# Zero products in TensorE's gaps, one engine for the later preparation, and earlier weight loads in a fused linear-attention and MLP kernel

## The chip, the cores and the metric

The kernel runs on one core of one Trainium2 chip. The metric is device time in microseconds, the median of several runs. A profile of one execution is shown beside it; its span is the time between the first and the last recorded instruction. Engines: TensorE (PE; PEld is its weight load), VectorE (DVE), ScalarE (ACT), GpSimd (POOL), SyncE (SP, which here only issues DMAs).

## The reference

Two parts follow one another: a recurrent linear attention with a per-channel decay, and an MLP with a squared ReLU.

```python
# attention: batch 4, heads 8, sequence 768, head_dim 48
for t in range(S):
    cur = einsum('bhd,bhe->bhde', u * kt, vt)
    y[:, :, t] = einsum('bhd,bhde->bhe', rt, state + cur)
    state = w[None, :, :, None] * state + einsum('bhd,bhe->bhde', kt, vt)
# x: 3072 tokens x 384 (heads side by side)
h = x @ w_in                 # 384 -> 2048
g = maximum(h, 0) ** 2
out = g @ w_out              # 2048 -> 384
```

## The kernel before

The sequence is cut into 6 chunks of 128 steps; with 4 batches this makes 24 **units**, numbered n = 4 x chunk + batch. A unit takes its steps in this order:

- SyncE loads `kt`, `rt`, `vt` of [128, 8, 48] F32 (L209), five buffers each. One queue carries these loads and the stores of the output (L408), in order.
- Preparation: `rk` = r*k (L214, GpSimd only); `rku` = rk*u (L217); `kw` = k times a decay factor, into the padded bf16 tile `kp` (L220); `rw` = r times a decay factor, into `rp` (L223); `vb` = v in bf16 (ScalarE, L226); `du` = sum of rku (VectorE, L228); `dv` = v*du (L231). `rku`, `kw`, `rw` and `dv` may go to GpSimd or VectorE. There are three padded tiles each, so the names kp_77, kp_78, kp_79 are units 0, 1, 2 modulo 3, and likewise rp_74, rp_75, rp_76.
- TensorE transposes kp and rp into a bf16 PSUM tile (L241), ScalarE copies it out as `rkT` (L247), TensorE forms k v (L258) for the state; VectorE adds it to the old state (L268, L270), VectorE or GpSimd multiplies with the decay (L277), ScalarE casts it to bf16 (L279).
- TensorE forms the scores (L288) into two PSUM tiles `at0`, `at1`, VectorE masks them (L298, `AT`), TensorE forms y from the state and the scores (L308, L313), VectorE adds dv (L321, `yb`), TensorE transposes y (L331), ScalarE copies it to `xt` (L352).

The MLP runs over **groups** of units: units 0 and 1, units 2 and 3, then four units at a time. For each group 16 hidden chunks are formed: three products of 128 x 256 or 128 x 512 columns (L363), ReLU on VectorE (L374) or ScalarE (L376), square on ScalarE (L381) or GpSimd (L383). Then for each unit the output is summed over the 16 chunks in four parts of four products (L396), copied by ScalarE (L404) and stored.

The weights are cast to bf16 by DMAs that GpSimd issues, four parts of `w_in` (L187) and four of `w_out` (L191). Part i is ordered behind `rk` of unit `W_IN_AT[i]` or `W_OUT_AT[i]`.

The order on every engine is written by a **planner**, a list scheduler that runs when the program is built. Every step is an `Op` with a duration for each engine that may do it ("T" TensorE, "V" VectorE, "A" ScalarE, "P" GpSimd, "D" the DMA engines, "S" the stores), a due time (6.6 us per unit, `PACE`), its dependences and the buffers that it takes. The planner repeatedly places the step that can start first (ties by due time; an engine that is not a step's first one is charged 8 us). The instructions are then emitted in that order. Each engine runs its queue in order, so a step that waits holds everything behind it. PSUM has three rings: `a` (3 tiles, attention), `h` (3, hidden chunks), `o` (2, output); `ps_tile` opens a tile of a ring when the first product of a step is emitted.

Before all units, a short prologue builds the decay factors. `emit_wc` transposes the decay row `wrow` on TensorE (L166) and squares it seven times on VectorE (L171).

Of the kernel before, what the change touches and what calls it, by code (L numbers as in the profile page):

```python
# [8 lines left out]
F32 = mybir.dt.float32  # L9
BF16 = mybir.dt.bfloat16  # L10
# [5 lines left out]
def kernel(  # L16
# [11 lines left out]
    nc = tc.nc  # L28
# [15 lines left out]
    const = ctx.enter_context(tc.tile_pool(name="const", bufs=1))  # L44
    work = ctx.enter_context(tc.tile_pool(name="work", bufs=1))
    psum = ctx.enter_context(tc.tile_pool(name="psum", bufs=1, space=bass.MemoryType.PSUM))
# [5 lines left out]
        out=wb, in_=bass.AP(tensor=w.tensor, offset=w.offset, ap=[[0, 128], [1, HD]])  # L52
# [10 lines left out]


    class Op:
        __slots__ = ("eng", "key", "deps", "takes", "emit", "start", "end", "lat", "by", "home")

        def __init__(self, eng, key, deps, takes, emit, lat=0.15):
            self.eng, self.key, self.deps, self.takes, self.emit = eng, key, deps, takes, emit
# [8 lines left out]
    rings = {}  # L78
# [4 lines left out]
    def sb_ring(name, bufs, shape, dt):  # L83
        ring(name, bufs, lambda i: work.tile(shape, dt, name=name, tag=name, bufs=bufs))
# [4 lines left out]
    def op(eng, key, deps, emit, takes=(), uses=(), lat=0.15):  # L89
        o = Op(eng, key, [d for d in deps if d is not None], list(takes), emit, lat)  # L90
        for b in list(takes) + list(uses):
            b.users.append(o)
        ops.append(o)
        return o
# [2 lines left out]
        return Buf(ringname)  # L97

    NLOAD, NPADS = 5, 3
    sb_ring("kt", NLOAD, [C, H, D], F32)  # L100
    sb_ring("rt", NLOAD, [C, H, D], F32)
    sb_ring("vt", NLOAD, [C, H, D], F32)
# [17 lines left out]
    for nm in ("rp", "kp"):  # L120
        pads[nm] = []
        for i in range(NPADS):
            t = const.tile([C, H, PAD], BF16, name=f"{nm}{i}")
# [5 lines left out]

    def ps_tile(buf, shape, dt):  # L130
        buf.tile = psum.tile(shape, dt, name=f"ps_{buf.ring}", tag=f"ps_{buf.ring}", bufs=rings[buf.ring]["bufs"])
        return buf.tile


    iota_i = const.tile([128, 1], mybir.dt.int32)
# [26 lines left out]
        nc.scalar.activation(wr.rearrange("p h d -> p (h d)"), lnw, AF.Exp, scale=er)  # L162

    def emit_wc():
        wcol_p = psum.tile([128, NP], F32, name="ps_a", tag="ps_a", bufs=rings["a"]["bufs"])
        nc.tensor.transpose(wcol_p, wrow.rearrange("p i d -> p (i d)"), ident4)  # L166
        wcs = const.tile([128, NP], F32, name="wsq", bufs=2)
        nc.vector.tensor_copy(wcs, wcol_p)
        for _ in range(C.bit_length() - 1):
            sq = const.tile([128, NP], F32, name="wsq", bufs=2)  # L170
            nc.vector.tensor_tensor(sq, wcs, wcs, ALU.mult)  # L171
            wcs = sq
        for i in range(2):
            rows = slice(i * PAD, i * PAD + D)
            nc.vector.tensor_copy(wc[rows, :, i, :], wcs[rows, :, None].to_broadcast([D, NP, D]))

    nc.scalar.dma_start(
        out=ub, in_=bass.AP(tensor=u.tensor, offset=u.offset, ap=[[0, 128], [1, HD]])
    )
    o_wk = op({"A": 1.95}, -50, [], emit_wk, lat=0.0)  # L180
    o_wr = op({"A": 0.6}, -49, [o_wk], emit_wr)
# [15 lines left out]
    for n in range(NU):  # L197
        c, b = divmod(n, B)
        t0 = c * C
        q = dict(n=n)  # L200
        units.append(q)
        K = PACE * n
        bufs = {nm: take(nm) for nm in ("kt", "rt", "vt", "vb", "rk", "rku", "du", "dv", "kp", "rp", "rkT", "AT", "yb")}
        q["b"] = bufs
        T = lambda nm, bufs=bufs: bufs[nm].tile

        def load(e, q=q, b=b, t0=t0, T=T):
            for nm, src in (("kt", k), ("rt", r), ("vt", v)):
                nc.sync.dma_start(out=T(nm), in_=src[b, :, t0 : t0 + C, :].rearrange("h t d -> t h d"))  # L209

        q["load"] = op({"D": 3.4}, K, [], load, takes=[bufs["kt"], bufs["rt"], bufs["vt"]], lat=1.4)
        two = lambda f: (lambda e: f({"P": nc.gpsimd, "V": nc.vector}[e]))
        q["rk"] = op({"P": 1.0}, K + 1, [q["load"]],
                     two(lambda e, T=T: e.tensor_tensor(T("rk"), T("rt"), T("kt"), ALU.mult)),  # L214
                     takes=[bufs["rk"]], uses=[bufs["rt"], bufs["kt"]])
        q["rku"] = op({"P": 1.0, "V": 0.47}, K + 2, [q["rk"]],
                      two(lambda e, T=T: e.tensor_tensor(T("rku"), T("rk"), ub, ALU.mult)),  # L217
                      takes=[bufs["rku"]], uses=[bufs["rk"]])
        q["kw"] = op({"P": 1.0, "V": 0.47}, K + 0.1, [q["load"], o_wk],
                     two(lambda e, T=T: e.tensor_tensor(T("kp")[:, :, :D], T("kt"), wk, ALU.mult)),  # L220
                     takes=[bufs["kp"]], uses=[bufs["kt"]])
        q["rw"] = op({"P": 1.0, "V": 0.47}, K + 0.2, [q["load"], o_wr],
                     two(lambda e, T=T: e.tensor_tensor(T("rp")[:, :, :D], T("rt"), wr, ALU.mult)),  # L223
                     takes=[bufs["rp"]], uses=[bufs["rt"]])
        q["vb"] = op({"A": 0.51}, K + 0.3, [q["load"]],
                     lambda e, T=T: nc.scalar.copy(T("vb"), T("vt")), takes=[bufs["vb"]], uses=[bufs["vt"]])  # L226
        q["du"] = op({"V": 0.55}, K + 3, [q["rku"]],
                     lambda e, T=T: nc.vector.tensor_reduce(T("du"), T("rku"), axis=mybir.AxisListType.X, op=ALU.add),  # L228
                     takes=[bufs["du"]], uses=[bufs["rku"]])
        q["dv"] = op({"P": 0.83, "V": 0.47}, K + 4, [q["du"], q["vb"]],  # L230
                     two(lambda e, T=T: e.tensor_tensor(T("dv"), T("vb"), T("du")[:, :, None].to_broadcast([C, H, D]), ALU.mult)),  # L231
                     takes=[bufs["dv"]], uses=[bufs["du"], bufs["vb"]])

# [16 lines left out]
        if not last:  # L250
            kv_p = take("a")
            sm = take(f"sm{b}")
            sb = take(f"sb{b}")

            def kvm(e, T=T, kv_p=kv_p):
                t = ps_tile(kv_p, [128, NP, 2, D], F32)
                for p in range(NP):
                    nc.tensor.matmul(  # L258
                        out=t[:, p], lhsT=T("kp")[:, 2 * p : 2 * p + 2, :],
                        rhs=T("vb")[:, 2 * p : 2 * p + 2, :], start=True, stop=True,  # L260
                    )

            q["kvm"] = op({"T": 0.2}, K + 1.2, [q["kw"], q["vb"], q["trr"]], kvm, takes=[kv_p, sm], uses=[bufs["kp"], bufs["vb"]], lat=0.3)
            old = units[n - B]["sm"] if c else None

            def sadd(e, kv_p=kv_p, sm=sm, old=old):
                if old is None:
                    nc.vector.tensor_tensor(sm.tile, kv_p.tile, wc, ALU.mult)  # L268
                else:
                    nc.vector.tensor_tensor(sm.tile, kv_p.tile, old.tile, ALU.add)  # L270

            q["sm"] = sm
            q["smo"] = op({"V": 0.55}, K + 3, [q["kvm"], units[n - B]["smo"] if c else None], sadd,
                          uses=[sm, kv_p] + ([old] if old else []))
            if c:
                q["smo"] = op({"P": 1.0, "V": 0.47}, K + 5, [q["smo"]],
                              two(lambda e, sm=sm: e.tensor_tensor(sm.tile, sm.tile, wc, ALU.mult)), uses=[sm])  # L277
            q["sbo"] = op({"A": 0.51}, K + 6, [q["smo"]],
                          lambda e, sm=sm, sb=sb: nc.scalar.copy(sb.tile, sm.tile), takes=[sb], uses=[sm])  # L279
            q["sb"] = sb  # L280
# [54 lines left out]

    groups = [[0, 1], [2, 3]] + [list(range(i, i + B)) for i in range(B, NU, B)]
    o_win, o_wout = [], []
    W_IN_AT, W_OUT_AT = (0, 1, 1, 2), (3, 4, 5, 6)
    for dst, when, part in ((o_win, W_IN_AT, w_in_part), (o_wout, W_OUT_AT, w_out_part)):
        for i in range(PARTS):  # L340
            key = PACE * when[i] + 1.1 + 0.01 * i
# [74 lines left out]
    while left:  # L416
        best = None
        for o in left:
            t = 0.0
            okay = True  # L420
            for d in o.deps:
                if d.end is None:
                    okay = False
                    break
                t = max(t, d.end + d.lat)
            if not okay:
                continue
            for bf in o.takes:
                rg = rings[bf.ring]
                same = [x for x in o.takes if x.ring == bf.ring]  # L430
                i = len(rg["order"]) + same.index(bf) - rg["bufs"]
                if i >= 0:
                    if i >= len(rg["order"]):
                        okay = False
                        break
                    for x in rg["order"][i].users:
                        if x.end is None:
                            okay = False
                            break
                        t = max(t, x.end + 0.1)  # L440
            if not okay:
                continue
            for e in o.eng:
                s = max(t, free[e])
                away = AWAY.get(e, 0.0) if len(o.eng) > 1 and e != o.home else 0.0
                rank = (s, o.key + away)
                if best is None or rank < best[0]:
                    best = (rank, o, e)
        (s, _), o, e = best
        o.start, o.end, o.by = s, s + o.eng[e], e  # L450
        free[e] = o.end
        for bf in o.takes:
            rings[bf.ring]["order"].append(bf)
        left.remove(o)
        placed.append(o)

    for o in placed:
        for bf in o.takes:
            rg = rings[bf.ring]
            if rg["make"] is not None:  # L460
                bf.tile = rg["make"](rg["order"].index(bf))
        o.emit(o.by)


# [28 lines left out]
```

## Time and profile before

| | us |
|---|---|
| median of 3 runs (lowest to highest) | 207.88 (207.57 to 207.95) |
| the profiled execution, whole | 206.22 |
| its span | 204.0 |
| TensorE busy (1529 products) | 175.2 |
| VectorE busy (260 instructions) | 153.5 |
| ScalarE busy (240) | 127.6 |
| GpSimd busy (136) | 126.3 |
| mean granted TensorE clock | 0.971 |

Busy times are of one execution, and a TensorE that is busy is not at its peak: products are pipelined and their recorded ends are modelled. Durations below come from this execution. Its whole time is 2.2 us longer than its span and 1.66 us shorter than the median.

The larger groups of the page (line, engine, operation, result and inputs, count, busy us, mean ns, idle before and what ended it):

```profile
L374 DVE TENSOR_SCALAR gr<-ps_h 128x512 f32<-128x512 f32 (+1 forms) x78 | 46.7, 609 | 26.4 <-PE ps_h L363 21.9
L298 DVE TENSOR_TENSOR AT<-ps_a,smask 128x512 bf16<-128x512 f32 x48 | 30.9, 679 | 2.7 <-PE ps_a L288 2.4
L214 POOL TENSOR_TENSOR rk<-rt,kt 128x384 f32<-128x384 f32 x24 | 27.3, 1144 | 4.5 <-DVE wsq L171 4.0
```

Other groups mix several buffers of one kind. The prediction takes the preparation steps from the windows instead.

### The profile page before, as it was taken

The page shows a single profiled execution, that of the slowest core. Times are in us where ns is not written, and L with a number is a line of the kernel's source. Part 1 is how long each engine was busy: PE and PEld are TensorE (multiplying, and loading weights), DVE is VectorE, ACT ScalarE, POOL GpSimd, SP SyncE. Part 2 cuts the span into 40 slices and gives each one's busy share as a digit, 9 for nine tenths or more (in the row PEclk, how much of TensorE's full clock was granted, in tenths as well). Part 3 has the DMA queues.
Part 4 walks back from the last instruction along what each step waited for, and adds up shares of the span by engine and source line. Part 5 has one row for each costly group of instructions (what it writes and reads, how often), then busy time and mean ns, then how long its engine had stood idle before and what let it go on. Part 6 is the DMA issues. An engine that isn't in the chain of part 4 may idle for free.

```text
span 204.0 us, 4084 instructions
## 1 busy us (share of the span) xinstructions
PE 175.2 (86%) x1529; PEld 106.4 (52%) x1529; DVE 153.5 (75%) x260; ACT 127.6 (63%) x240; POOL 126.3 (62%) x136
## 2 busy tenths in 40 slices
PE   0147893999599999977999999799999999999992
PEld 0135561576356656553565655465556655555551
DVE  4899689478859999899989999999764564455200
ACT  3536475569553997965988777687566755544211
POOL 2767489548899698999998899995322020422200
PEclk9999999589969999999999999999999999999998
DMA  5999999981519989989815661110111011111122
GB/s 113 205 198 195 194 201 174 219 146 26 70 45 233 244 163 216 194 203 183 160 41 117 150 121 42 39 39 3 39 39 42 0 39 43 39 39 39 42 77 77
DMA packets 82367, 22.68 MB, mean 111 GB/s; under 512 B 75436, under 2 KB 82348, under 8 KB 82348
## 3 DMA queue, kind: packets, MB, share of 16 engines
q1 hardware_dynamic: 78480, 19.08, 42.6%
q0 software_dynamic: 3712, 3.15, 10.4%
q8 instruction: 12, 0.20, 0.4%
q10 hardware_dynamic: 156, 0.20, 0.4%
q14 instruction: 7, 0.06, 0.1%
HBM read 20.84 MB, written 4.72 MB: 125 GB/s over the span
## 4 chain that ended last, share of the span: by engine, by line
PE 66%; DVE 20%; DMA 6%; issue 3%; POOL 3%; ACT 1%; POOLq 0%; DVEq 0%; ACTq 0%
PE ps_o L396 27%; PE ps_h L363 26%; DMA w_out_sb<-in_moe_w_out_dram 4%; PE ps_a L241 4%; DVE AT L298 3%; PE ps_a L288 3%; PE ps_a L313 2%; DMA wrow<-in_w_dram 2%; DVE rku L217 2%; DVE gr L374 2%; PE ps_a L331 2%; PE ps_a L308 2%; DVE dv L231 2%; DVE rp_75 L223 1%; DVE yb L321 1%
## 5 line engine op out<-in xcount | busy, mean ns | idle before, releaser
L374 DVE TENSOR_SCALAR gr<-ps_h 128x512 f32<-128x512 f32 (+1 forms) x78 | 46.7, 609 | 26.4 <-PE ps_h L363 21.9
L363 PEld LDWEIGHTS <-w_in_sb 128*128 128x128 bf16 x336 | 31.2, 101 | 22.7 <-issue 3.0
L298 DVE TENSOR_TENSOR AT<-ps_a,smask 128x512 bf16<-128x512 f32 x48 | 30.9, 679 | 2.7 <-PE ps_a L288 2.4
L214 POOL TENSOR_TENSOR rk<-rt,kt 128x384 f32<-128x384 f32 x24 | 27.3, 1144 | 4.5 <-DVE wsq L171 4.0
L247 ACT COPY rkT<-ps_a 128x1024 bf16<-128x1024 bf16 x24 | 24.2, 1010 | 6.1 <-PE ps_a L241 6.1
L376 ACT ACTIVATE gr<-ps_h 128x512 f32<-128x512 f32 (+1 forms) x34 | 17.8, 532 | 8.0 <-PE ps_h L363 7.6
L404 ACT COPY osb<-ps_o 128x384 f32<-128x384 f32 x24 | 11.4, 475 | 15.2 <-PE ps_o L396 15.0
L383 POOL TENSOR_TENSOR g_2830<-gr 128x512 bf16<-128x512 f32 x5 | 5.2, 1039 | 20.6 <-DVE gr L374 20.6
L231 POOL TENSOR_TENSOR dv<-vb,du 128x384 f32<-128x384 bf16 x16 | 13.7, 857 | 5.4 <-DVE yb L321 2.4
L321 DVE TENSOR_TENSOR yb<-ps_a,dv 128x384 bf16<-128x384 f32 x24 | 13.1, 548 | 2.0 <-PE ps_a L313 2.0
L313 PE MATMUL ps_a<-vb,AT 128*128 128x48 bf16 x192 | 12.6, 190 | 1.5 <-DVE AT L298 1.5
L363 PE MATMUL ps_h<-xt_1214,w_in_sb 128*128 128x512 bf16 x48 | 12.5, 379 | 1.2 <-DVE gr L374 1.2
L288 PE MATMUL ps_a<-rkT 48*128 48x128 bf16 x192 | 10.7, 233 | 3.1 <-ACT rkT L247 3.1
L396 PE MATMUL ps_o<-w_out_sb,g_2035 128*128 128x384 bf16 x64 | 13.0, 326 | 0.0
L228 DVE TENSOR_REDUCE du<-rku 128x8 f32<-128x384 f32 x24 | 12.9, 539 | 0.1
L396 PE MATMUL ps_o<-w_out_sb,g_1046 128*128 128x384 bf16 x64 | 12.9, 326 | 0.0
L313 PEld LDWEIGHTS <-AT 128*128 128x128 bf16 x192 | 10.6, 101 | 4.3 <-DVE AT L298 2.3
L396 PE MATMUL ps_o<-w_out_sb,g_2479 128*128 128x384 bf16 x64 | 12.9, 326 | 0.0
L363 PE MATMUL ps_h<-xt_2112,w_in_sb 128*128 128x512 bf16 x48 | 12.8, 379 | 0.0
L363 PE MATMUL ps_h<-xt_2535,w_in_sb 128*128 128x512 bf16 x48 | 12.8, 379 | 0.0
L363 PE MATMUL ps_h<-xt_1707,w_in_sb 128*128 128x512 bf16 x48 | 12.7, 380 | 0.0
L396 PE MATMUL ps_o<-w_out_sb,g_1578 128*128 128x384 bf16 x64 | 12.5, 326 | 0.0
(180 smaller groups left out, 404.7 us busy)
## 6 DMA issues: line engine op xcount, KB each, us to landing
kt<-in_k_dram SPq DMA_DIRECT2D x24, 192.0 KB, 3.7
rt<-in_r_dram SPq DMA_DIRECT2D x24, 192.0 KB, 3.7
vt<-in_v_dram SPq DMA_DIRECT2D x24, 192.0 KB, 4.2
out_dram<-osb SPq DMA_DIRECT2D x24, 192.0 KB, 1.9
w_in_sb<-in_moe_w_in_dram POOLq DMA_DIRECT2D x4, 384.0 KB, 6.3
w_out_sb<-in_moe_w_out_dram POOLq DMA_DIRECT2D x4, 384.0 KB, 6.9
wb<-in_w_dram SPq DMA_DIRECT2D x1, 192.0 KB, 3.6
ub<-in_u_dram ACTq DMA_DIRECT2D x1, 192.0 KB, 3.9
```

What stands on the lines that cost most here:

```text
L214: two(lambda e, T=T: e.tensor_tensor(T("rk"), T("rt"), T("kt"), ALU.mult)),
L228: lambda e, T=T: nc.vector.tensor_reduce(T("du"), T("rku"), axis=mybir.AxisListType.X, op=ALU.add),
L231: two(lambda e, T=T: e.tensor_tensor(T("dv"), T("vb"), T("du")[:, :, None].to_broadcast([C, H, D]), ALU.mult)),
L247: lambda e, T=T, rk_p=rk_p: nc.scalar.copy(T("rkT"), rk_p.tile),
L288: nc.tensor.matmul(out=ts[i][:, p, :], lhsT=T("rkT")[rows, p, 1, :], rhs=T("rkT")[rows, p, 0, :], start=True, stop=True,)
L298: lambda e, T=T, i=i, x=x: nc.vector.tensor_tensor(T("AT")[:, i], x.tile, smask[:, None, :].to_broadcast([128, NP, C]), ALU.mult),
L313: nc.tensor.matmul(out=t[:, p, i, :], lhsT=T("AT")[:, i, p, :], rhs=T("vb")[:, 2 * p + i, :], start=st is None, stop=True, skip_group_chec ...
L321: lambda e, T=T, y_p=y_p: nc.vector.tensor_tensor(T("yb"), y_p.tile.rearrange("t p i d -> t (p i d)"), T("dv").rearrange("t h d -> t (h d) ...
L363: nc.tensor.matmul(out=t, lhsT=w_in_sb[:, kk, f * 128 : (f + 1) * 128], rhs=xt.tile[:, kk].rearrange("p b t -> p (b t)"), start=(kk == 0), ...
L374: nc.vector.tensor_scalar(gr.tile[:, : L * C], h.tile, 0.0, None, ALU.max)
L376: nc.scalar.activation(gr.tile[:, : L * C], h.tile, AF.Relu)
L396: nc.tensor.matmul(out=o_p.tile, lhsT=g.tile[:, f, j, :], rhs=w_out_sb[:, f, :], start=(f == 0), stop=(f == NF - 1),)
```

## The change

There are four edits.

1. A tile `zb` of zeros is set once. `warm` emits products of zeros into a given PSUM tile. In the prologue nine of them (`WARM0`) go ahead of the transpose of `wrow` and six (`WARM1`) behind it, into a tile of ring `a` of their own.
2. The planner notes for each TensorE step, if it is placed before 70 us of its own time, the gap that TensorE has in front of it. When such a step opens an F32 PSUM tile, `int(gap * 0.6 / 0.2133)` zero products are emitted into that tile first. The step's own first product starts the sum afresh. A step that opens two tiles (the scores) emits them for each. Steps that open a bf16 tile or none get no zeros.
3. For units from 8 on, `rku`, `kw`, `rw`, `dv` and the decay of the state are offered to GpSimd only. For units 0 to 7 VectorE's duration in the planner goes from 0.47 to 0.6.
4. The parts of w_in are ordered behind units 0, 0, 1, 1 instead of 0, 1, 1, 2, those of w_out behind 3, 3, 4, 4 instead of 3, 4, 5, 6.

```diff
+    WARM0, WARM1 = 9, 6
+    WARM_END = 70.0
+    NDVE = 8
...
     def ps_tile(buf, shape, dt):
         buf.tile = psum.tile(shape, dt, name=f"ps_{buf.ring}", tag=f"ps_{buf.ring}", bufs=rings[buf.ring]["bufs"])
+        if dt == F32 and now["gap"] > 0:
+            warm(buf.tile, shape, int(now["gap"] * FILL / 0.2133))
         return buf.tile
+    FILL = 0.6
+    now = dict(gap=0.0)
+    zb = const.tile([128, 512], BF16)
+    nc.vector.memset(zb, 0.0)
+
+    def warm(tile_, shape, count):
+        dims = list(shape[1:])
+        for _ in range(count):
+            nc.tensor.matmul(
+                out=tile_, lhsT=zb[:, :128], rhs=view(zb, dims), start=True, stop=True, skip_group_check=True
+            )
...
     def emit_wc():
+        first = psum.tile([128, 512], F32, name="ps_a", tag="ps_a", bufs=rings["a"]["bufs"])
+        warm(first, [128, 512], WARM0)
         wcol_p = psum.tile([128, NP], F32, name="ps_a", tag="ps_a", bufs=rings["a"]["bufs"])
         nc.tensor.transpose(wcol_p, wrow.rearrange("p i d -> p (i d)"), ident4)
+        warm(first, [128, 512], WARM1)
...
+        both = (lambda p_, v_, n=n: {"P": p_, "V": v_} if n < NDVE else {"P": p_})
...
-        q["rku"] = op({"P": 1.0, "V": 0.47}, K + 2, [q["rk"]],
+        q["rku"] = op(both(1.0, 0.6), K + 2, [q["rk"]],
...
-        q["dv"] = op({"P": 0.83, "V": 0.47}, K + 4, [q["du"], q["vb"]],
+        q["dv"] = op(both(0.83, 0.6), K + 4, [q["du"], q["vb"]],
...
-    W_IN_AT, W_OUT_AT = (0, 1, 1, 2), (3, 4, 5, 6)
+    W_IN_AT, W_OUT_AT = (0, 0, 1, 1), (3, 3, 4, 4)
...
         o.start, o.end, o.by = s, s + o.eng[e], e
+        o.gap = s - free[e] if e == "T" and s < WARM_END else 0.0
...
+        now["gap"] = o.gap
         o.emit(o.by)
```

`kw`, `rw` and the decay of the state (L277) are changed like `rku`. `view` gives the zeros the shape of the tile.

More of the change, by code (lines that the diff above doesn't have):

```diff
@@ L65 @@
     class Op:
-        __slots__ = ("eng", "key", "deps", "takes", "emit", "start", "end", "lat", "by", "home")
+        __slots__ = ("eng", "key", "deps", "takes", "emit", "start", "end", "lat", "by", "home", "gap")
         def __init__(self, eng, key, deps, takes, emit, lat=0.15):
@@ L131, in ps_tile, with view @@
         buf.tile = psum.tile(shape, dt, name=f"ps_{buf.ring}", tag=f"ps_{buf.ring}", bufs=rings[buf.ring]["bufs"])
+        if dt == F32 and now["gap"] > 0:
+            warm(buf.tile, shape, int(now["gap"] * FILL / 0.2133))
         return buf.tile
+    FILL = 0.6
[8 more added lines that the diff above has]
+            )
+    def view(t, dims):
+        cols = 1
+        for d in dims:
+            cols *= d
+        if len(dims) == 1:
+            return t[:, :cols]
+        if len(dims) == 2:
+            return t[:, :cols].rearrange("p (a b) -> p a b", a=dims[0])
+        return t[:, :cols].rearrange("p (a b c) -> p a b c", a=dims[0], b=dims[1])
     iota_i = const.tile([128, 1], mybir.dt.int32)
@@ L215 @@
                      takes=[bufs["rk"]], uses=[bufs["rt"], bufs["kt"]])
-        q["rku"] = op({"P": 1.0, "V": 0.47}, K + 2, [q["rk"]],
+        q["rku"] = op(both(1.0, 0.6), K + 2, [q["rk"]],
                       two(lambda e, T=T: e.tensor_tensor(T("rku"), T("rk"), ub, ALU.mult)),
                       takes=[bufs["rku"]], uses=[bufs["rk"]])
-        q["kw"] = op({"P": 1.0, "V": 0.47}, K + 0.1, [q["load"], o_wk],
+        q["kw"] = op(both(1.0, 0.6), K + 0.1, [q["load"], o_wk],
                      two(lambda e, T=T: e.tensor_tensor(T("kp")[:, :, :D], T("kt"), wk, ALU.mult)),
                      takes=[bufs["kp"]], uses=[bufs["kt"]])
-        q["rw"] = op({"P": 1.0, "V": 0.47}, K + 0.2, [q["load"], o_wr],
+        q["rw"] = op(both(1.0, 0.6), K + 0.2, [q["load"], o_wr],
                      two(lambda e, T=T: e.tensor_tensor(T("rp")[:, :, :D], T("rt"), wr, ALU.mult)),
@@ L275 @@
             if c:
-                q["smo"] = op({"P": 1.0, "V": 0.47}, K + 5, [q["smo"]],
+                q["smo"] = op(both(1.0, 0.6), K + 5, [q["smo"]],
                               two(lambda e, sm=sm: e.tensor_tensor(sm.tile, sm.tile, wc, ALU.mult)), uses=[sm])
```

## The prediction

> **What bounds the kernel now.** I read the page's 40 slices first, then the chain that ended last, then windows, waits and single instructions. Columns of a slice row: one digit per 5.1 us.
>
> ```profile
> PE   0147893999599999977999999799999999999992
> DVE  4899689478859999899989999999764564455200
> POOL 2767489548899698999998899995322020422200
> PEclk9999999589969999999999999999999999999998
> ...
> PE 66%; DVE 20%; DMA 6%; issue 3%; POOL 3%; ACT 1%; POOLq 0%; DVEq 0%; ACTq 0%
> ```
>
> There are three stages. Up to about 66 us TensorE works with holes, and twice at half clock. From 66 to 145 us TensorE, VectorE and GpSimd are all near full. From 145 us TensorE alone is full, with nothing to win there. Two thirds of the chain is TensorE.
>
> How much TensorE could save follows from its own rates. In the chain a hidden-layer chunk of three 512-column products takes 0.65 us, and the last 64 output products take 10.54 us (0.165 each). After 66 us there are five groups: 5 x (16 x 0.65 + 10.54) = 104.7, and sixteen units of attention at about 1.6 (the products of one unit laid end to end at full clock) = 25.6; together 130. The last product ends at 200.4, so 134.4 us are spent and about 4 are lost. The whole program is 130 + 35 = 165 us of products; with the first at 9.64, some 22 us are lost before 66 us. That is where most can be had.
>
> Windows: start:end, length, then PE, PEld, DVE, ACT, POOL busy with counts, clock, DMA share, GB/s.
>
> ```profile
> 35.00:36.00 1.00, 0.31 (x4) 0.31 (x5) 1.00 (x3) 0.00 (x0) 0.49 (x1) 0.66 1.21 204
> 36.00:37.00 1.00, 1.00 (x12) 0.94 (x11) 0.12 (x2) 0.77 (x2) 0.00 (x0) 0.50 1.36 242
> 41.00:42.00 1.00, 1.00 (x6) 0.61 (x5) 0.86 (x2) 0.38 (x1) 1.00 (x2) 0.50 0.43 83
> 58.00:59.00 1.00, 1.00 (x5) 0.48 (x4) 1.00 (x2) 0.00 (x0) 0.72 (x1) 0.50 0.00 0
> 90.00:95.00 5.00, 4.06 (x36) 2.31 (x37) 5.00 (x8) 2.81 (x4) 4.67 (x4) 1.00 0.90 216
> 95.00:100.00 5.00, 3.75 (x38) 2.29 (x37) 5.00 (x10) 3.60 (x7) 4.58 (x6) 1.00 1.05 209
> ```
>
> From 35.7 to 42.1 and from 55.9 to 59.1 us the clock is 0.50 while TensorE is busy (6.0 and 3.1 us of work): full clock would save 3.0 + 1.6 = 4.6 us. The start is slow as well, though the clock column says 1.00: nine 256-column products took 2.08 us at 22.3 and nine took 1.23 us at 24.7. In the 5-us windows from 85 to 135 the idle of TensorE sums to 3.9 us; VectorE is full there.
>
> **1. Units from 8 on: GpSimd alone.** In the stretch 61 to 150 us VectorE did 31 of these optional steps: 8 rku, 7 kw, 8 rw, 6 dv, 2 sm, in 6.16 + 7.85 + 6.89 + 6.54 + 2.53 = 30.0 us. The row of kw, VectorE first and GpSimd behind:
>
> ```profile
> 61.00:150.00 89.00, 7.85 (x7) 8.59 (x8) 1.00 0.58 126
> ```
>
> VectorE needs 1.12 us here, against 0.54 in its shortest runs of the same step; GpSimd 1.07 against 0.99. The Trainium skill speaks against the move: GPSIMD Engine Reference, section 4.1, gives elementwise work of two inputs to VectorE, GpSimd being about 2x slower. By that rule VectorE is relieved of 31 x 0.55 = 17 us and GpSimd loaded with 30: a loss of 13 engine-us. By the rows VectorE is relieved of 30 us and GpSimd takes 25 x 1.0 + 6 x 0.83 = 30, an even trade, because two-input steps stretch while GpSimd runs (SBUF — State Buffer, on the shared port pair, calls it a lock for a whole instruction). I take the row.
>
> GpSimd's sum in 61 to 150: about 76 now + 30 - 14.1 (12 squares that ScalarE does at 0.61, 7.4 us on an engine 74% busy) - 5 (its own stretching gone) = 87 of 89 us. Per unit it is 4 x 1.0 + 0.83 + 1.0 = 5.83 us, under TensorE's 27.3 / 4 = 6.8. So GpSimd is full and just fast enough. VectorE falls from 97% to some 65%, and the chain's pieces of kw, rw, rku and dv on VectorE at 87 to 95 us disappear. Of the 3.9 us idle I leave 1.0 for other waits: **-2.9 us** (bounds 0 and -3.9; the other sign is rival C).
>
> **2. Zero products.** The memset of zb (some 0.3 us on VectorE, by the 0.27 us of its neighbours) lies in VectorE's idle time before 5.4 us. Nine products at half clock cost 9 x 0.427 = 3.84 us (twice 0.2133) from about 1.4 us, and the first transpose waits for wrow until 5.15 anyway: at most 0.1. Six more end by 8.0, before the 9.64 of unit 0's transposes: hidden by 1.6 us.
>
> The rest stands only ahead of products that open an F32 tile. What TensorE waited for up to 60 us (line, releaser: total, times, longest):
>
> ```profile
> PE ps_a L241 <- DVE kp_77 L220: 4.3, 1, 4.3
> PE ps_a L288 <- ACT rkT L247: 3.1, 5, 0.9
> PE ps_a L331 <- DVE yb L321: 2.1, 3, 1.4
> PE ps_a L241 <- DVE sm_177 L268: 2.0, 1, 2.0
> PE ps_a L313 <- DVE AT L298: 1.3, 3, 0.5
> ```
>
> L241 and L331 are transposes into bf16 tiles: no zeros there. That leaves L288 (3.1), L313 (1.3) and L363 and L396 (0.9): 5.3 x 0.6 / 0.2133 = 15 products, and L288 opens two tiles and gets its count twice: about 24, or 5 us. The idle that the 5-us windows show from 5 to 70 us, 16.2 us, would give 45 as an upper bound. Where the real wait is shorter than the planned one a zero product costs 0.216 on the path. I charge **+1.0** (a fifth of them; bounds 0 and +5).
>
> Will they hold the clock? TensorE: Matmul & The Clock Gate, Part 1, says that the clock halves after an idle window of about 3.4 us. By that rule one product in each window holds it, and all 4.6 us come. The trace differs: between 32.2 and 35.6 us TensorE ran products for about 0.9 us in pieces (the last of L313, four transposes at 33.85) and the clock still fell. So about a quarter busy is too little, and the holes ahead of transposes, which made both falls, stay unfilled. I take half of 4.6, **-2.3** (bounds 0 and -4.6), and for the cold start **-1.0**: between 14 and 24 us the chain holds 4.5 us of slow products, worth 2.1 at full clock, but units 1 and 2 wait for VectorE and for loads at 1.1 DMA share as well (bounds 0 and -2.1).
>
> **3. Weights earlier.** The last part of w_out decides when output products end:
>
> ```profile
> 51.95 0.80 POOL L191 DMA_DIRECT2D w_out_sb<-in_moe_w_out_dram  x1
> 57.71 2.19 PE L396 MATMUL ps_o<-w_out_sb,g_333 128*128 128x384 bf16 x8
> 59.71 0.36 SPq L408 DMA_DIRECT2D out_dram<-osb  x1
> 60.16 0.39 SPq L209 DMA_DIRECT2D kt<-in_k_dram  x1
> ```
>
> It is issued behind unit 6's rk; the products follow at 57.7, and SP, in order, holds unit 9's loads behind unit 0's store. With unit 4's rk (40.5) the last part goes 11 us earlier. TensorE idles 2.6 us between 52.9 and 57.1; products of groups 0 and 1 can go there, and next late is the chain of unit 7 (kw, rw on VectorE until 55.8). I take **-1.0** (bounds 0 and -2.6). Price: the GpSimd issue is still 8 x 0.80. w_in's second part goes ahead of unit 1's kw, 0.8 us, hidden behind VectorE's rw of unit 1 until 13.9 (0.8 if not); w_out's second passes unit 4's kw and rk (up to 0.8). On the 16 DMA engines a weight part takes 10.4% x 204 / 8 = 2.65 us; two parts pushed ahead delay the loads of units 5 to 7 by up to 5.3 us, which now are issued 6 to 15 us before their first use: hidden.
>
> The dearer prices that the planner now gives VectorE (0.6 for 0.47) push early steps to GpSimd, which had 9 us of waits between 35 and 53: nothing.
>
> **Sum.** -2.9 + 1.0 - 2.3 - 1.0 - 1.0 = -6.2. The profiled execution is 206.22 us (span 204.0 and 2.2 around it), so 200.0 for it; the median of the runs is 207.88, 1.66 above, so **201.7 us** there.
>
> **Rivals.** A is the above: 55%. B: only the middle gains; the waits for preparation swallow the clock: 207.9 - 2.9 = 205.0. For it: the unfilled holes, and a TensorE that after 42 us soon waits for units 6 and 7. Against it: GpSimd's idle at 43 to 46 and 46.6 to 47.2 us waited for results of TensorE, so faster products pull preparation along. 16%. C, the other side: GpSimd becomes the bound. From 6.8 us per unit on it decides; 5.83 plus one wait of 1.4 per unit (its wait for du or the state sum was 2.4 and 1.7 us in single cases) makes 7.2, and sixteen units make 16 x 0.4 = 6.4 us, less 2.3 from the clock: 212. For it: no other engine may help and 87 of 89 us are spoken for. Against it: the stretching ends, and units were prepared by 148 us, with 50 us of TensorE work left. 19%. D: zeros on the path, 45 x 0.216 = 9.7 us, half of it exposed against -3.9 of the rest: 209. For it: the count comes from planned gaps, and the attention products get theirs twice. Against it: TensorE's largest waits are not filled at all. 10%.
>
> **Numbers.** A measurement of this kernel tells about 0.2% (0.4 us) from no change. Faster takes A, nearly all of B and a little of D: 0.73. Same 0.04. Slower: C and most of D, 0.23. For A alone 198 to 204.5. The range goes to B and D and part of C: 196.5 to 210.5.
>
> **What will show it.** VectorE's rows of kw, rw, rku, dv after 62 us should be gone and GpSimd's be at 1.0; TensorE's idle in 85 to 135 us under 1.5; the slices of the clock at 35 to 42 and 55 to 59 us fuller; zero products 25 to 60 besides the first 15; w_out's last issue before 43 us; the first 512-column hidden products (now 65.9) at 60 to 63. GpSimd steps over 1.1 us or waits of TensorE on GpSimd's kw and rw after 80 us would make it wrong; so would L288 later by the length of its zeros.

## The result and the profile after

| | before | after |
|---|---|---|
| median of 4 runs, us | 207.72 (206.92 to 207.95) | 202.70 (202.32 to 202.89) |
| ratio, 95% interval | | 0.9763 (0.9732 to 0.9793) |
| profiled execution / its span, us | 206.22 / 204.0 | 202.89 / 201.1 |
| products on TensorE | 1529 | 1565 |
| VectorE / GpSimd busy, us | 153.5 / 126.3 | 134.0 / 135.2 |

The change makes the kernel 2.4% faster: 5.0 us between the medians, 3.3 us between the two profiled executions. Times are medians of all executions, but a ratio leaves out those that were over 1.5% slower than the fastest of their kernel, so it can differ a little from the quotient of two medians. Line numbers after L99 move with the change: transposes L241 are now L274, scores L288 are L321, hidden chunks L363 are L396, outputs L396 are L429, the preparation lines L214 to L231 are L247 to L264.

The 40 slices of the changed kernel (5.0 us each):

```profile
PE   7474798696699799999999999999999999999992
...
DVE  5896868279976787896988558887476564555200
...
POOL 2665918279969999999998999989984010422200
PEclk9976559999999999999999999999999999999999
```

Read them against the rows before. From about 70 us TensorE has nothing but nines; the dips at 87 to 97 and 127 to 133 us are gone. VectorE, which stood at nine there, has room, and GpSimd is at nine until 150 us. But the first fourteen slices look no better. The half-clock stretches at 36 to 42 and 56 to 59 us are gone, and a longer one, from 16.3 to 30 us, has come, with a short one at 9.5 to 12.9 ahead of it. In windows of the changed kernel (16 to 30 at half clock, 35 to 42 at full):

```profile
16.00:30.00 14.00, 10.18 (x88) 7.44 (x85) 9.23 (x19) 6.14 (x14) 7.43 (x10) 0.51 1.11 198
35.00:42.00 7.00, 5.25 (x41) 3.80 (x41) 2.16 (x5) 3.27 (x9) 2.37 (x5) 1.00 1.07 187
```

The clock row is silent about the start: it shows full clock until the first change on record, which came at 25.1 us before and at 6.1 us after. The products tell it. Before, those of 256 columns followed one another every 0.21 us up to 25.1 us and every 0.11 from there. After, the zeros of 512 columns came every 0.43 us up to 5.9 and every 0.22 from 6.2 us on. With the start counted, the time at half clock fell from 35.3 to 23.1 us (the mean clock of 0.971 before leaves the slow start out).

All the same, the start gained nothing. The first hidden chunk of 512 columns starts at 70.3 us, 4.4 us later than before, in part because other products went ahead of it: at 75 us TensorE has 122.5 us of products left, against 121.4 before, so the changed kernel is about 1 us behind. From there the order of the finish turns round. The first products of the following groups stand at 92.2, 116.1, 142.0 and 167.3 us, against 92.5, 117.8, 144.6 and 170.2. The windows 85 to 150 us, before first, changed kernel second:

```profile
85.00:150.00 65.00, 61.08 (x587) 36.08 (x586) 61.05 (x98) 49.63 (x92) 54.32 (x51) 1.00 0.42 93
```

```profile
85.00:150.00 65.00, 65.00 (x626) 39.06 (x623) 49.12 (x85) 54.30 (x101) 62.14 (x67) 1.00 0.45 101
```

TensorE idled 3.9 us of 65 before and not at all after. Less the 1 us lost in the start, this is the whole of the 2.9 us between the two spans. The 5.0 us between the medians hold some 2 us more, which these two executions don't show: the profiled one of before was 1.5 us under its median. VectorE fell from 61 to 49 us. kw in 61 to 150 us shows what became of a preparation step, VectorE's share first, then GpSimd's (changed kernel):

```profile
61.00:150.00 89.00, 0.00 (x0) 15.89 (x16) 1.00 0.59 129
```

All sixteen ran on GpSimd at 0.99 us; before, seven ran on VectorE at 1.12 and eight on GpSimd at 1.07.

### The profile page after: what moved, and what is told of

Read it like the earlier page. It is cut to its first block, busy times and chain, and to the rows that moved or that the text cites. A ratio compares the mean times of both kernels' runs of the same rounds, so it can differ in the third digit from the quotient of the medians.

```text
span 201.1 us, 4167 instructions
## 1 busy us (share of the span) xinstructions
PE 180.6 (90%) x1565; PEld 108.8 (54%) x1565; DVE 134.0 (67%) x239; ACT 128.7 (64%) x243; POOL 135.2 (67%) x155
## 4 chain that ended last, share of the span: by engine, by line
PE 70%; DMA 9%; DVE 7%; POOL 5%; SPq 4%; issue 2%; ACT 1%; POOLq 0%; DVEq 0%; ACTq 0%
PE ps_h L396 28%; PE ps_o L429 28%; DMA rt<-in_r_dram 4%; PE ps_a L274 4%; DMA w_out_sb<-in_moe_w_out_dram 4%; SPq L241 4%; PE ps_a L321 3%; PE ps_a L364 2%; PE ps_a L346 2%; PE ps_a L341 2%; DVE AT L331 2%; PE ps_a L291 1%; POOL rk L247 1%; DVE rku L250 1%; POOL rku L250 1%
## 5 line engine op out<-in xcount | busy, mean ns | idle before, releaser
L407 DVE TENSOR_SCALAR gr<-ps_h 128x512 f32<-128x512 f32 (+1 forms) x84 | 51.7, 624 | 35.8 <-PE ps_h L396 30.9
L396 PEld LDWEIGHTS <-w_in_sb 128*128 128x128 bf16 x336 | 31.6, 100 | 20.6 <-issue 0.6
L331 DVE TENSOR_TENSOR AT<-ps_a,smask 128x512 bf16<-128x512 f32 x48 | 30.8, 682 | 3.8 <-PE ps_a L321 3.7
L247 POOL TENSOR_TENSOR rk<-rt,kt 128x384 f32<-128x384 f32 x24 | 25.4, 1062 | 6.0 <-DVE wsq L203 3.9
L250 POOL TENSOR_TENSOR rku<-rk,ub 128x384 f32<-128x384 f32 x20 | 20.2, 1008 | 0.3
L264 POOL TENSOR_TENSOR dv<-vb,du 128x384 f32<-128x384 bf16 x21 | 17.6, 840 | 3.9 <-DVE du L261 3.0
L409 ACT ACTIVATE gr<-ps_h 128x512 f32<-128x512 f32 (+1 forms) x28 | 13.8, 502 | 9.6 <-PE ps_h L396 9.2
L259 ACT CAST vb<-vt 128x384 bf16<-128x384 f32 x24 | 12.1, 509 | 7.7 <-DMA vt<-in_v_dram 7.7
L149 PE MATMUL ps_a<-zb 128*128 128x512 bf16 (+1 forms) x28 | 10.6, 503 | 2.8 <-DVE zb L144 1.3
L429 PE MATMUL ps_o<-w_out_sb,g_2038 128*128 128x384 bf16 x64 | 13.0, 326 | 0.0
L429 PE MATMUL ps_o<-w_out_sb,g_1578 128*128 128x384 bf16 x64 | 12.9, 326 | 0.0
L429 PE MATMUL ps_o<-w_out_sb,g_2501 128*128 128x384 bf16 x64 | 12.9, 326 | 0.0
L396 PE MATMUL ps_h<-xt_2120,w_in_sb 128*128 128x512 bf16 x48 | 12.8, 379 | 0.0
L396 PE MATMUL ps_h<-xt_2624,w_in_sb 128*128 128x512 bf16 x48 | 12.8, 379 | 0.0
L429 PE MATMUL ps_o<-w_out_sb,g_1150 128*128 128x384 bf16 x64 | 12.7, 326 | 0.0
L396 PE MATMUL ps_h<-xt_1681,w_in_sb 128*128 128x512 bf16 x48 | 12.7, 379 | 0.0
L414 ACT ACTIVATE g_2501<-gr 128x512 bf16<-128x512 f32 x15 | 9.5, 633 | 4.8 <-DVE gr L407 4.6
```

The lines of the kernel that those rows point to most:

```text
L331: lambda e, T=T, i=i, x=x: nc.vector.tensor_tensor(T("AT")[:, i], x.tile, smask[:, None, :].to_broadcast([128, NP, C]), ALU.mult),
L396: nc.tensor.matmul(out=t, lhsT=w_in_sb[:, kk, f * 128 : (f + 1) * 128], rhs=xt.tile[:, kk].rearrange("p b t -> p (b t)"), start=(kk == 0), ...
L407: nc.vector.tensor_scalar(gr.tile[:, : L * C], h.tile, 0.0, None, ALU.max)
L409: nc.scalar.activation(gr.tile[:, : L * C], h.tile, AF.Relu)
L429: nc.tensor.matmul(out=o_p.tile, lhsT=g.tile[:, f, j, :], rhs=w_out_sb[:, f, :], start=(f == 0), stop=(f == NF - 1),)
```

## The experiments

All runs were compared with the kernel before, run on the same chip beside them. The spread of single runs is about 1%, so a ratio is known to some 0.5%, and differences under 1 us between two experiments are not told apart.

**The third edit alone, and all but the third.** In e1 only the preparation edit is kept.

```diff
-    WARM0, WARM1 = 9, 6
+    WARM0, WARM1 = 0, 0
-    FILL = 0.6
+    FILL = 0.0
-    W_IN_AT, W_OUT_AT = (0, 0, 1, 1), (3, 3, 4, 4)
+    W_IN_AT, W_OUT_AT = (0, 1, 1, 2), (3, 4, 5, 6)
```

> Only the third edit: units from 8 on prepared by GpSimd, VectorE priced 0.6 for units 0 to 7; no zero products, the old order of weights. If the middle of the program is what pays: 203 to 204.5 us (3 to 4.5 under before, the 3.9 us in which TensorE idled between 85 and 135), with the two stretches at half clock still there. If the clock or the weights pay: within 1 us of before.

In e2 the preparation is as before (prices included), zeros and weights as in the changed kernel.

```diff
-    NDVE = 8
+    NDVE = 24
-both(1.0, 0.6)   and both(0.83, 0.6)
+both(1.0, 0.47)  and both(0.83, 0.47)
```

> Edits 1, 2 and 4 (zeros and weights) with the old preparation on both engines. If the middle pays: 206 to 208, TensorE idle again 3 to 4 us between 85 and 135. If the start pays, by clock or weights: 203 to 204.5.

Measured: e1 203.42 us, ratio 0.9823 (0.978 to 0.9866); e2 211.8 us, ratio 1.0255 (1.0209 to 1.03). The preparation edit alone brings 1.8%. Without it the other three edits together don't gain: they cost 2.6%, more than e2's expectation had for the worst case. In e1 TensorE's idle between 85 and 150 us is zero, as in the changed kernel, while its clock still halves twice:

```profile
PEclk9999999699966999999999999999999999999999
```

**Without zeros, and with the old weights.** e3 is the changed kernel with the zeros set to none as above; e4 is the changed kernel with the old `W_IN_AT` and `W_OUT_AT`.

> The changed kernel without any zero product. If the zeros hold the clock and this is worth something: 2 to 3 us slower than the changed kernel (205 to 206), with stretches at half clock near 35 and 56 us. If they only take turns with the real products: 202 to 203, or 1 us faster than the changed kernel.

> The changed kernel with the weights back at units 0, 1, 1, 2 and 3, 4, 5, 6. If the earlier weights are worth the 1 us that the prediction gave them: 203.7. If they only exchange one wait for another (the loads of units 2 and 3 for w_in): 202.2 to 203.2.

Measured: e3 202.61 us, 0.9769 (0.973 to 0.9807); e4 202.92 us, 0.9777 (0.9732 to 0.9823). Neither differs from the changed kernel (0.9763) by more than its interval: leaving the zeros out costs nothing that can be told, and e4 lies where its expectation put weights that only exchange one wait for another. The slices of e3 show what the zeros do to the clock:

```profile
PEclk9999999997999799999999999999999999999999
```

Without zeros the row is at half from 47.4 to 50.8 and from 67.8 to 71.3 us; with them from 9.5 to 12.9 and 16.3 to 30.0 us. The start, of which neither row tells, has to be added. In e3 the 256-column products still take 0.21 us each until 26.9 us:

```profile
25.36 1.88 PE L396 MATMUL ps_h<-xt,w_in_sb 128*128 128x256 bf16 x9
...
27.25 0.82 PE L396 MATMUL ps_h<-xt,w_in_sb 128*128 128x256 bf16 x6
```

So the zeros end the slow start at 6.1 instead of 26.9 us and bring slow time later. In sum the half clock falls from 33.7 to 23.1 us, and products other than zeros run in it for 10.6 instead of 16.6 us. The zeros do hold the clock better; the time doesn't follow.

**Each of the others alone.** e5 keeps only the zeros, e6 only the weights, e7 only VectorE's new price (0.6 for all units, `NDVE = 24`).

> Only edits 1 and 2, the zero products, in the kernel before; preparation, prices and weights as before. Edits 1, 2 and 4 together (with the new prices) took 4.9 us more than before. If the zeros alone make that: 210 to 212. If they are as neutral here as in the changed kernel: 206.5 to 208.

> Only edit 4, the earlier weights, in the kernel before. If the weights make the 4.9 us loss seen with the old preparation (the loads of units 2 and 3 pushed back by w_in): 209 to 212. If they are neutral: 206.5 to 208. The prediction's own estimate was 1 us faster: 206.

> Only the planner's price of VectorE, 0.6 for 0.47, for all units, in the kernel before; nothing else. If the gain of the third edit comes from the price (another order, not another engine): 203 to 204.5. If it comes from GpSimd alone preparing units from 8 on: within 1 us of before.

(e5's expectation says that e2 had the new prices; by its edit it had the old ones.)

Measured: e5 206.43 us, 0.9945 (0.9906 to 0.9984); e6 213.86 us, 1.0323 (1.0282 to 1.0364); e7 203.87 us, 0.9811 (0.9765 to 0.9858). Two surprises. The earlier weights alone cost 3.2%. And the price alone, which only makes the planner choose otherwise, brings as much as the whole preparation edit. The window 85 to 150 us of e7, in an execution of 206.18 us, 2.3 above its median:

```profile
85.00:150.00 65.00, 63.43 (x607) 38.52 (x605) 60.51 (x98) 49.80 (x90) 60.12 (x58) 1.00 0.43 96
```

VectorE is as full as before (60.5 of 65 us), and still TensorE idles only 1.6 us instead of 3.9. So "VectorE is full" was not by itself what stopped TensorE. It may depend on which steps stand in VectorE's queue ahead of those that TensorE waits for; no run tests that alone.

In e6 a single step shows how badly that can go. VectorE's rows first, then GpSimd's, 43 to 49 us (start, duration, engine, line):

```profile
43.59 0.54 DVE L303 TENSOR_TENSOR sm<-ps_a,sm 128x384 f32<-128x384 f32 x1
...
44.39 4.62 DVE L310 TENSOR_TENSOR sm<-sm,wc 128x384 f32<-128x384 f32 x1
48.94 0.68 DVE L331 TENSOR_TENSOR AT<-ps_a,smask 128x512 bf16<-128x512 f32 x1
```

```profile
43.97 0.85 POOL L264 TENSOR_TENSOR dv<-vb,du 128x384 f32<-128x384 bf16 x1
44.76 1.00 POOL L253 TENSOR_TENSOR kp<-kt,wk 128x384 bf16<-128x384 f32 x1
45.71 0.99 POOL L256 TENSOR_TENSOR rp<-rt,wr 128x384 bf16<-128x384 f32 x1
46.66 1.93 POOL L247 TENSOR_TENSOR rk<-rt,kt 128x384 f32<-128x384 f32 x2
48.67 1.20 POOL L250 TENSOR_TENSOR rku<-rk,ub 128x384 f32<-128x384 f32 x1
```

The decay of the state, 0.55 us when VectorE has it undisturbed, is recorded for 4.62 us. It ends only after GpSimd's unbroken run of five instructions (dv, kp, rp and two rk) has ended at 48.59; that GpSimd's next, an rku, then takes 1.20 us for 1.0 fits a turn given to VectorE there. The mask (L331) waits behind it, TensorE waits 4.62 us for the mask, and is busy for 0.27 of the 5 us from 45 to 50.

**The mirror.** In e8 the optional steps from unit 8 on go to VectorE alone.

```diff
-{"P": p_, "V": v_} if n < NDVE else {"P": p_}
+{"P": p_, "V": v_} if n < NDVE else {"V": v_}
```

> The mirror of the third edit: rku, kw, rw, dv and the state's decay of units from 8 on are offered to VectorE only, GpSimd keeps rk and squares; no zeros, old weights. By the Trainium skill's page GPSIMD Engine Reference, section 4.1 (two-input work belongs on VectorE), this relieves GpSimd at a small price and should be as fast as the third edit alone or faster: 202 to 204. By the rows (a two-input step on VectorE stretches to about 1.1 us when GpSimd runs beside it) VectorE has about 3 + 5 x 0.6 to 1.0 us per unit plus ReLUs, which is at or over TensorE's 6.8: 206 to 212.

Measured: 207.59 us, 1.0045 (1.0001 to 1.009). TensorE idles 3.1 us between 85 and 150 us with VectorE at 63.1 of 65. The steps cost VectorE about 0.8 us each there (between 85 and 135 us 37 of them take 28.6 us), between the 0.55 of the rule and the 0.97 of the row before: with GpSimd busy for 40 us instead of 54 they meet it less often. The rule that gives two-input work to VectorE loses here, it seems because VectorE's own share leaves no room for it. (The planner also moved other work: in e8 VectorE ran 6 of the ReLUs between 85 and 150 us, against 21 before, and still was full.)

**Price, rule and weights crossed.** Three more runs without zeros, so that the three choices can be read against each other. e9: GpSimd alone from 8, old price, old weights. e10: new price for all units (`NDVE = 24`), new weights. e11: GpSimd alone from 8, old price, new weights.

> GpSimd alone from unit 8 on, but VectorE still priced at 0.47 for units 0 to 7; no zeros, old weights. The price alone gave a ratio of 0.981 and price and rule together 0.982. If the rule works by itself, by taking VectorE's idle-making load out of the middle: 203 to 204.5, and TensorE idle under 0.5 us between 85 and 135. If only the price works: 206 to 208.

> Price 0.6 for all units and the earlier weights; VectorE may still prepare units from 8 on; no zeros. Weights alone cost 3.2%. If that loss is a VectorE step held out by a run of GpSimd instructions (4.62 us at 44 us for the state's decay), a new price that moves steps may avoid it: 203 to 206. If the earlier weights cost by themselves with the old preparation: 209 to 212.

> GpSimd alone from unit 8 on and the earlier weights, VectorE at 0.47 for units 0 to 7; no zeros. The rule changes nothing planned before unit 8, so the step held out at 44 us should be there again: if that hold-out is the loss, 207 to 210, with TensorE idle some 4 us at 45 to 50; if the rule alone makes the gain whatever the start does: 202 to 204.

| ratio to before, no zeros | old weights | new weights |
|---|---|---|
| old preparation | 1 | 1.0323 (e6) |
| new price only | 0.9811 (e7) | 1.0113 (1.0058 to 1.0167) (e10) |
| GpSimd alone from 8 only | 0.981 (0.975 to 0.9869) (e9) | 0.9949 (0.9916 to 0.9981) (e11) |
| both, as in the change | 0.9823 (e1) | 0.9769 (e3) |

e9's expectation for the rule holds in time (203.09 us). TensorE waits once between 85 and 150 us there, for 0.8 us, more than expected; another 0.6 us without products lies where the trace lacks some. Rule and price each bring 1.9% and together no more. The right column is the other finding. With any preparation but the full new one the earlier weights cost 1.4 to 3.2%; with it they cost nothing and may bring 0.5%. The step held out for 4.6 us is there in e6, e2 and e11 and not in e10 nor e3. It doesn't explain the column by itself: e10 avoids it and is still 3% slower than e7, with TensorE busy for only 1.97 of the 5 us from 65 to 70. Most of the loss lies in the start: at 75 us TensorE has 121.4 us of products left before, 122.1 in e3, but 125.4 in e10 and e11 and 129.4 in e6 (part of it at half clock in e6 and e10).

**A further step.** e12 is e3 (no zeros, new weights) with GpSimd alone from unit 4 on (`NDVE = 4`).

> The changed kernel without zeros (202.6 us) with GpSimd alone from unit 4 on. If VectorE steps held out in units 4 to 7 (0.9 to 1.35 us each between 44 and 56 us) cost time there: 200 to 202. If GpSimd, full between 45 and 70 us already, is then the bound: 204 to 208.

Measured: 206.54 us, 0.9984 (0.9945 to 1.0024), 4 us slower than e3. GpSimd is busy for 29.8 of the 30 us from 40 to 70, VectorE for 15.3 and TensorE for only 3.0 of 5 us at 60 to 65 and again at 65 to 70. So the choice of 8 matters: one group earlier GpSimd is full and TensorE starves beside it, as rival C feared.

None of the experiments beats the changed kernel clearly; e3, without zeros, equals it.

## Why the prediction was right, point by point

The forecast of 201.7 us is 1.0 under the measured 202.7 and in its range, in part by luck. Adding the edits in the order preparation, weights, zeros, the ratios give e1 0.9823, e3 0.9769, changed kernel 0.9763: of 207 us that is -3.7, -1.1 and -0.1. By way of e4 the zeros come to -1.0 and the weights to -0.3, so the two can't be told apart; together they are -1.2, hardly more than the noise. The prediction had -2.9 for the preparation and -3.3 for these two. One term was too small and the other too large. Nor do the terms stand for themselves: put last, behind the other edits (e2), the preparation is worth 4.8%.

1. **GpSimd alone from 8 (-2.9): the mechanism right in its effect, and shown.** The idle of TensorE between 85 and 150 us went from 3.9 to zero, and e1 alone does it; I had left 1.0 for other waits. GpSimd's steps fell to 1.0 us and it stayed just fast enough, busy for 86.0 of the 89 us from 61 to 150, where the sum had 87. VectorE fell to 76% (85 to 150 us) and not to some 65, since it took over ReLUs: 31 there, 21 before. The sum by rows (an even trade of 30 us) was nearer than the rule's loss of 13 engine-us, and e8 confirms the side. But the reading "VectorE is full, so relieve it" was too simple: e7 gains the same 1.9% with VectorE as full as before. The planner took VectorE's step at 0.47 us, the trace has 0.97. Both the rule and the price work against that error, which may be why they don't add; this is argued, not shown.

2. **The clock (-2.3 and -1.0), zeros on the path (+1.0): the clock rose, and the time did not follow.** "I take half of 4.6" and "for the cold start -1.0" should have been next to nothing. The two named stretches did go to full clock, and the start from 6.1 us on, but 9.5 to 12.9 and 16.3 to 30 us were at half, the latter with products in 10.2 of 14 us. In each of the four pairs of runs without and with zeros, TensorE ran less of its real work at half clock (profiled executions, the start up to the first change of the clock counted as half; e5's was 2.7 us above its median):

   | without, with zeros | products other than zeros at half clock, us | change of the ratio |
   |---|---|---|
   | before, e5 | 20.0, 12.0 | -0.55% |
   | e6, e2 | 23.7, 15.7 | -0.7% |
   | e1, e4 | 20.4, 12.2 | -0.5% |
   | e3, changed kernel | 16.6, 10.6 | -0.1% |

   Six to eight us less at half clock would save 3 to 4 us at most, if TensorE set the time there. Measured are 0.45% on average, about 0.9 us, and only the first two pairs are just clear of noise. So the step that failed is to count slow products as lost time. That waits for loads and preparation swallow the rest, as rival B said, is read from the chains and not tested: unit 2's `rt` lands at 18.0 us in the changed kernel and at 17.7 in e3, and both have unit 2's `yb` behind it, at 25.9 and 25.6. (The cold start's sum was also short: the chain has over 5 us of products there, where I counted 4.5.)

   Nor was the clock held all through. The holes ahead of the transposes, 2.6 us at 7.2 to 9.8 and 2.4 us at 16.7 to 19.1, got no zeros, as I said: the clock fell in the first, and stayed down through the second. But it fell at 16.3, ahead of that hole, after 3.4 us with 2.0 us of products, a zero among them, so thinly filled gaps are not enough either.

   The count was near: 15 and 21 more, where I had 24 by the waits and 45 at most. The charge of 1.0 for zeros on the path was met in one place. Unit 0's `rkT` is ready at 11.90 us; the scores start only behind the last of four zeros, 1.0 us later (0.06 in e3). One more zero stands in the chain that ended last, at 67.8. What these delays cost in the end is not shown.

```profile
10.89 1.01 ACT L280 COPY rkT<-ps_a 128x1024 bf16<-128x1024 bf16 x1 [2.96 <-PE ps_a L274]
10.98 1.99 PE L149 MATMUL ps_a<-zb 128*128 128x512 bf16 x4
12.90 0.40 PE L321 MATMUL ps_a<-rkT 48*128 48x128 bf16 x8
```

3. **Weights (-1.0): not shown to be worth anything, at a price that I called hidden.** They bring 0.3 us beside the zeros (e4) and 1.1 without (e1, e3), both within the noise. Nor did all parts go earlier. Issued before and after, in us: w_in 8.4, 11.7, 17.7, 21.6 and 8.5, 9.5, 20.5, 22.1; w_out 30.6, 34.7, 41.4, 52.0 and 29.9, 30.7, 45.2, 46.0. I priced the push of unit 1's kw (0.8 us) and the loads of units 5 to 7. I did not price w_in's second part against unit 2's load: both parts are now issued at 8.5 to 10.2 us, and GpSimd and VectorE wait for unit 2's `rt` until 18.0, where GpSimd waited until 15.5 before. Then the chain runs as follows (changed kernel; start, duration, what):

```profile
9.18 8.82 DMA rt<-in_r_dram
18.06 0.44 issue
18.50 0.56 DVE yb L354
19.10 1.01 PE ps_a L274 x8
```

   The larger price is another. I read the rk at 40.5 us as unit 4's; it was unit 5's, and unit 4's ran at 33.8. In the changed kernel it starts at 43.4, though its loads have landed by 23.6: GpSimd works in order, and squares of the second group stand in front and wait for their ReLUs (GpSimd's rows; kp_78 is unit 4's here):

```profile
38.53 1.27 POOL L416 TENSOR_TENSOR g_573<-gr 128x256 bf16<-128x256 f32 x2 [3.12 <-DVE gr L407]
41.22 1.27 POOL L416 TENSOR_TENSOR g_573<-gr 128x256 bf16<-128x256 f32 x2 [1.43 <-DVE gr L407]
42.45 1.00 POOL L253 TENSOR_TENSOR kp_78<-kt,wk 128x384 bf16<-128x384 f32 x1
43.41 1.32 POOL L247 TENSOR_TENSOR rk<-rt,kt 128x384 f32<-128x384 f32 x1
```

   All runs divide by this. Unit 4's rk starts at 33.8 to 36.6 us in every run with the old weights and at 40.5 to 43.4 in every run with the earlier ones. So w_out's last part, behind it, came 6 us earlier and not 11; unit 0's store went out at 56.5 instead of 59.7 us. Rivals of the other sign were all about GpSimd or the zeros; that this harmless-looking edit alone costs 3.2% with the old preparation was in none of them. It stays open why the full new preparation makes up for the late unit 4 (e3) while that of e10 does not.

4. **Signs that I named.** Right: kw, rw and rku from 8 on gone from VectorE, GpSimd's at 1.0, no idle of TensorE in 85 to 135, full clock at 35 to 42 and 55 to 59, no waits on GpSimd after 80 us. Wrong: the first 512-column products at 60 to 63 (70.3), w_out before 43 (46.0), 25 to 60 zeros besides the first 15 (21); unit 0's scores came later by their zeros, one of the signs against me.

**Rivals.** B (only the middle gains, 205.0) described the mechanism best and was too slow by 2.3 us: the preparation gave 0.8 us more (e1), and the rest is the 1.2 us of weights and zeros with the noise. C did not come at 8 but does at 4 (e12). D came only in unit 0's scores: with zeros no pair got slower.

## What to carry to other kernels

Price a step in a planner by what it takes beside its neighbours, not alone: correcting 0.47 to 0.6 us was worth as much here as assigning the steps by hand. Filling an engine's gaps to hold its clock pays only where that engine sets the time: here six to eight us less of slow products were worth about one. Edits to one planned order don't add: test each with and without the others, since one that is free beside the new preparation cost 3% beside the old. And where engines work in order, ask what a moved step now stands behind.

## What the hardware showed that was not expected

A VectorE step with two SBUF inputs was held out not for one GpSimd instruction but through five in a row: 4.62 us for 0.55 (e6, with the same step at 4.63 in e2 and e11), and 2.59 us through three in the kernel before (32.57 us). SBUF — State Buffer in the Trainium skill (two separate sides) describes the shared port pair as going to whichever starts first, for a whole instruction. In these traces the waiting VectorE step did not get its turn between two GpSimd instructions.

The granted clock changed only in steps of 3.4 us: in the changed kernel at 6.1, 9.5, 12.9, 16.3 and 30.0 us. It fell to half at 9.5, 2.3 us after the zeros had ended at 7.2, behind a step (6.1 to 9.5) with 1.1 us of products; and again at 16.3 behind a step with 2.0 us of products:

```profile
7.30:9.50 2.20, 0.00 (x0) 0.00 (x0) 2.05 (x6) 0.63 (x2) 1.89 (x3) 1.00 0.98 196
...
12.90:16.30 3.40, 2.00 (x36) 1.48 (x37) 3.15 (x5) 1.52 (x2) 1.61 (x2) 1.00 1.20 195
```

Busy time alone doesn't decide: in e3 the clock fell behind a step with 2.2 us of products (64.4 to 67.8), in e4 it held through one with 1.6 (8.4 to 11.8). The page TensorE: Matmul & The Clock Gate, Part 1, speaks of an idle window of about 3.4 us. The length agrees with the steps here; but no step ahead of these falls was idle, and the measurement decides.
